# One matrix load per unit, and the next expert's first token blocks transposed one unit earlier

## The chip, the cores and the metric

The kernel runs on one core of a Trainium2 chip. The metric is the device time of one execution in microseconds (us), and the median of several runs is compared.

## The reference

Three stages follow one another on 4608 tokens of 512 numbers. Only the second, the mixture of experts, is touched.

```python
attn_out = _attn_ref(**attn_kwargs)                 # 8 batches, 8 heads, 576 x 64, keys and values pooled by 8
x = attn_out.transpose(0, 2, 1, 3).reshape(B * S, H * D)
...
# second stage: each token goes to its two best experts of eight
for e in range(E):
    for k in range(2):
        mask = top2[:, k] == e
        h = np.maximum(x[mask] @ w1[e], 0.0)        # 512 -> 1024
        out[mask] += top2_w[mask, k, None] * (h @ w2[e])   # 1024 -> 512
...
h = x @ w_in                                        # third stage, 512 -> 2048 -> 512
g = h - np.tanh(h)
return g @ w_out
```

## The kernel before

The second stage walks over 8 experts. An expert has room for 1216 tokens, which are worked on in three groups of 512, 384 and 320 tokens. A group takes 8 units, one for each 128 columns of the expert's hidden layer, so an expert has 24 units, counted here from 0 to 23: units 0 to 7 are the 512 group, 8 to 15 the 384 group, 16 to 23 the 320 group. Numbers are carried as a high and a low half in 16 bits, so a product is three matmuls.

A unit does this, in the order in which the code issues it: `L1(i, f)` multiplies the group's transposed tokens `xTp` with the first matrix (lines 355 to 357, result in `ph`, two buffers), ScalarE (ACT) and VectorE (DVE) turn `ph` into the hidden tile `hT` (lines 359 and 360); then at most one token block of the next group is transposed by `tr`; then `L2` of two units ago multiplies `hT` with the second matrix (lines 377 to 384, result in `py`); at a group's end `Y` scales the `py` tiles into `ys` (three buffers) and stores them to `y_d` (line 409); then the jobs that a table gives to this unit are run (`at` enters them, `run_jobs` issues them).

`tr` works on a block of up to 128 tokens that `gather` has fetched into `xg`. ACT makes the high half in the single buffer `xp` (line 341), DVE the low half (line 342), SyncE's queue (SP) issues a transposing DMA from `xp` into `xTp` (line 343), and GpSimd (POOL) gathers the block after next. `xTp` has two buffers, so a new group's tile takes the place of the tile of two groups before. TensorE (PE) needs all blocks of a group before its first matmul. A group of four blocks had `tr` in units 0, 2, 4 and 6 of the group before it, a group of three in 0, 2 and 5.

Among the jobs of the table: the next expert's first matrix is loaded into `stage` (line 118, four DMAs of 512 KB), its largest entry is found (`amax`, line 127, units 3 to 6, in expert 0 four later), and it is split into halves in `pair` (lines 154 and 159); from unit 13 the same `stage` takes the second matrix (line 120). Meanwhile a piece of the third stage's matrices is loaded (`raw`, lines 225 and 228) and converted. In experts 1 to 4, units 1 and 2, four sums of such pieces are split (lines 290 and 291) into the same three `ys` buffers and stored to `ws_d` (line 293).

All ordinary DMAs here and the transposes go through SP, which issues in program order. A unit's order on each engine is the order of the code; no scheduler moves it.

Of the kernel before, what the change touches and what calls it, by code (L numbers as in the profile page):

```python
# [37 lines left out]
def kernel(ctx, tc, q, k, v, w_gate, w_noise, noise, w1, w2, w_in, w_out, out):  # L38
# [54 lines left out]
    with ExitStack() as st:  # L93
        moe(nc, tc, st, V, z)
# [81 lines left out]
def both(g):  # L176
    for _ in g:
        pass
# [8 lines left out]
def moe(nc, tc, st, V, z):  # L187
# [8 lines left out]
    KD, KF = DM // 128, FF // 128  # L196
# [6 lines left out]
    groups = []  # L203
    for e in range(E):
        c = 0
# [91 lines left out]
    def at(key, f, *a):  # L297
        jobs.setdefault(key, []).append((f, a))

    def run_jobs(key, between):  # L300
        for f, a in jobs.pop(key, []):
            f(*a)
            between()
# [3 lines left out]
    def gather(k):  # L307
        if k < len(blocks):
            e, c, n = blocks[k]
            if k == 6:  # L310
                x = wk.tile([128, 2, DM], F16, name="xp", bufs=1).rearrange("p a n -> p (a n)").bitcast(F32)
            else:
                x = wk.tile([128, DM], F32, name="xg", bufs=2)
            XG[k] = x
            nc.gpsimd.indirect_dma_start(  # L315
                out=x[:n], out_offset=None, in_=x_d[:, :],
                in_offset=bass.IndirectOffsetOnAxis(ap=idx[:n, e, c:c + 1], axis=0))
# [7 lines left out]
    def tr(i, j):  # L325
        if j == 0:
            XTP[i] = wk.tile([128, 2, KD, 512], F16, name="xTp")
        x = XG.pop(first[i] + j)
        n = blocks[first[i] + j][2]
        if i == 1:  # L330
            p = ps.tile([128, KD, 128], F32, name="pt", bufs=2)
            for m in range(KD):
                nc.tensor.transpose(p[:, m, :n], x[:n, 128 * m:128 * m + 128], identf[:n, :n])
            o = XTP[i][:, :, :, 128 * j:128 * j + n]
            nc.scalar.activation(o[:, 0], p[:, :, :n], AF.Copy)
            tt(o[:, 1], p[:, :, :n], o[:, 0], op=OP.subtract)  # L336
            if j < 2:
                gather(7 + j)
            return
        xp = wk.tile([128, 2, DM], F16, name="xp", bufs=1)  # L340
        nc.scalar.activation(xp[:n, 0], x[:n], AF.Copy)
        tt(xp[:n, 1], x[:n], xp[:n, 0], op=OP.subtract)  # L342
        nc.sync.dma_start_transpose(XTP[i].rearrange("p a m n -> p (a m) n")[:, :, 128 * j:128 * j + n],
                                    xp[:n].rearrange("p a n -> p (a n)"))
        gather(first[i] + j + 2)
# [3 lines left out]
    def L1(i, f):  # L349
        e, g, c0, nt = groups[i]  # L350
        w, x = W[e, 1].pair, XTP[i]
        p = ps.tile([128, 512], F32, name="ph", bufs=2)
        for m in range(KD):
            s = slice(128 * f, 128 * f + 128)
            nc.tensor.matmul(p[:, :nt], w[:, 0, m, s], x[:, 0, m, :nt], start=(m == 0), stop=False)  # L355
            nc.tensor.matmul(p[:, :nt], w[:, 0, m, s], x[:, 1, m, :nt], start=False, stop=False)  # L356
            nc.tensor.matmul(p[:, :nt], w[:, 1, m, s], x[:, 0, m, :nt], start=False, stop=(m == KD - 1))  # L357
        h = HC[i, f] = wk.tile([128, 2, 512], F16, name="hT", bufs=5)
        nc.scalar.activation(h[:, 0, :nt], p[:, :nt], AF.Relu)  # L359
        stt(h[:, 1, :nt], p[:, :nt], 0.0, h[:, 0, :nt], op0=OP.max, op1=OP.subtract)  # L360
# [3 lines left out]
    def L2(i, f):  # L364
        e, g, c0, n = groups[i]
        w, h = W[e, 2].pair.rearrange("p a b (c n) -> p a (b c) n", n=DM), HC[i, f]
        nb, half = divmod(n, 128)
        if f == 0:
            if g == 0:
                SC[e] = wk.tile([128, 1], F32, name="ysc")  # L370
                tt(SC[e], W[e, 1].sc[:, 1:2], W[e, 2].sc[:, 0:1], op=OP.mult)
            for j in range(nb + (half > 0)):
                PY[i, j] = ps.tile([128, DM], F32, name="py", bufs=4)
        for j in range(nb):
            s = slice(128 * j, 128 * j + 128)
            p = PY[i, j]
            nc.tensor.matmul(p, h[:, 0, s], w[:, 0, f], start=(f == 0), stop=False)  # L377
            nc.tensor.matmul(p, h[:, 0, s], w[:, 1, f], start=False, stop=False)  # L378
            nc.tensor.matmul(p, h[:, 1, s], w[:, 0, f], start=False, stop=(f == KF - 1))  # L379
        if half and f % 2:  # L380
            terms = [(u, a, b) for u in (f - 1, f) for a, b in ((0, 0), (0, 1), (1, 0))]
            for k, (u, a, b) in enumerate(terms):
                q = 64 * (k % 2)
                nc.tensor.matmul(PY[i, nb][q:q + 64], HC[i, u][:, a, 128 * nb:n], w[:, b, u],
                                 start=(f == 1 and k < 2), stop=(f == KF - 1 and k > 3))
        if not half:
            del HC[i, f]
        elif f % 2:
            del HC[i, f - 1], HC[i, f]
        if f == KF - 1 and i > 0:  # L390
            Y(i)
# [161 lines left out]
    for e in range(E):  # L553
        if e + 1 < E:
            c1, c2 = PR[e + 1, 1], PR[e + 1, 2]
            d = 4 if e == 0 else 0
            at((e, d), c1.load)
            at((e, 7 + d), lambda c=c1: both(c.fin1()))
            at((e, 8 + d), lambda c=c1: both(c.fin2()))
            for c in range(4):  # L560
                at((e, 3 + d + c), c1.amax, c)
                at((e, (12 if d else 10) + c), c1.split, c)
                at((e, 18 + c // 2), c2.amax, c)
                at((e, 22 + c // 2), c2.split, c)
            at((e, 15 if d else 13), c2.load)
            at((e, 20), lambda c=c2: both(c.fin1()))
            at((e, 21), lambda c=c2: both(c.fin2()))
        cv = Conv(e // 4, e % 4)
        for j in range(8):
            u = j + 3 if 0 < e < 5 else (j + 2 if j < 6 else j + 4) if e + 1 < E else (j + 4 if j < 5 else j + 6)  # L570
            if j < 2:
                at((e, j + 2 * (e + 1 == E)), cv.load, j)
            at((e, u), cv.conv, j)
            if j + 2 < 8:
                at((e, u), cv.load, j + 2)
        at((e, 14), cv.stat)
        at((e, 15), cv.fin1)
        at((e, 16), cv.fin2)
        at((e, 16), cv.norm)
        for j in range(4):  # L580
            at((e, 20 + j // 2), cv.split, j)
            if cv.which == 0:
                if j == 0:
                    at((e + 1, 0), cv.combos)
                at((e + 1, 1 + j // 2), cv.split, j, True)
# [11 lines left out]
    for u in range(len(units) + LAG):  # L597
        if u < len(units):
            i, f = units[u]
            L1(i, f)  # L600
            if u < KF:
                gate(4)
            n = -(-groups[i + 1][3] // 128) if i + 1 < len(groups) else 0
            if i > 0:
                for j in range(n):
                    if j * KF // n == f:
                        tr(i + 1, j)
            elif f == KF - 1:
                while not V["idx_loaded"]:
                    gate(10 ** 6, True)  # L610
                for k in range(4, 7):
                    gather(k)
        if u >= LAG and u not in (KF, KF + 1):
            L2(*units[u - LAG])
        if u == KF - 1:
            L2(*units[u - 1])
            L2(*units[u])
            for j in range(n):
                tr(1, j)
        if u in (KF, KF + 1):  # L620
            Y(0, range(2 * (u - KF), 2 * (u - KF) + 2))
        if u > LAG and units[u - LAG - 1][1] == KF - 1 and groups[units[u - LAG - 1][0]][0:2] == (E - 2, len(SIZES) - 1):
            overflow()
        if u in (1, 3):
            V["first"][1].split((u + 3) // 2)
        if u < KF:
            gate(6, u > 1)
        if u == KF + LAG:
            V["early"].close()
            V["pairs"].append(V["ew"].enter_context(tc.tile_pool(name="ew1", bufs=1, side="right")))  # L630
        if u < len(units):
            run_jobs((groups[i][0], KF * groups[i][1] + f), lambda: u < KF and gate(4))
            if u < KF:
                gate(6)
# [1096 lines left out]
```

## Time and profile before

| | |
|---|---|
| median of 3 runs | 1812.55 us (1811.64 to 1812.95) |
| the profiled execution's own time | 1809.6 us |
| its span, first to last instruction | 1807.6 us |
| PE busy | 1754.3 us, 97% |
| DVE, ACT, POOL busy | 1282.7, 940.8, 277.6 us |
| granted TensorE clock, mean | 0.997 |

Busy PE time counts a matmul from its start to its modelled end. Matmuls overlap, so a wait shows as idle time only after the last one's modelled end.

### The profile page before, as it was taken

To read this page: it belongs to the slowest core of one execution; us is meant where nothing else is said; L and a number is where in the kernel's file an instruction comes from. 1 tells how busy PE (TensorE), PEld (TensorE's weight loads), DVE (VectorE), ACT (ScalarE), POOL (GpSimd) and SP (SyncE) were. 2 spreads that over 40 slices of the span, in tenths; PEclk is the share of its full clock that TensorE was granted. 3 is DMA by queue.
4 is the path that set the end of the run, shared out by engine and by line. 5 is a ranking of instruction groups with operands and counts; after the bars stand their busy time and mean duration, and the time that the engine had idled before them with its cause. 6 is when DMAs were issued, how large, how long until landed. Compare 5 with 4: busy or idle time off the path is not lost. (4 is left out here: it accounts for less than half of the span.)

```text
span 1807.6 us, 28937 instructions
## 1 busy us (share of the span) xinstructions
PE 1754.3 (97%) x10791; PEld 1069.2 (59%) x10792; DVE 1282.7 (71%) x2550; ACT 940.8 (52%) x2249; POOL 277.6 (15%) x264
## 2 busy tenths in 40 slices
PE   7999989999999999999999999999999999999998
PEld 5998854445454454545455454566666666666664
DVE  5688786766666766665665457687887879788765
ACT  5887732424434343434334246566665756666554
POOL 2334101302121130100101012010120201010000
PEclk8999999999999999999999999999999999999999
DMA  9867214454655445454634335430322314041100
GB/s 240 220 172 211 79 59 149 120 166 140 198 152 143 131 120 177 140 149 129 149 102 123 100 101 140 103 89 23 94 65 48 95 34 94 18 94 46 37 25 25
DMA packets 264158, 203.45 MB, mean 113 GB/s; under 512 B 188160, under 2 KB 208640, under 8 KB 264000
## 3 DMA queue, kind: packets, MB, share of 16 engines
q1 hardware_dynamic: 251840, 162.16, 33.1%
q0 software_dynamic: 11904, 38.81, 8.2%
q8 instruction: 89, 1.46, 0.3%
q14 instruction: 69, 0.57, 0.1%
q10 hardware_dynamic: 256, 0.46, 0.1%
HBM read 121.82 MB, written 45.74 MB: 93 GB/s over the span
## 5 line engine op out<-in xcount | busy, mean ns | idle before, releaser
L359 ACT ACTIVATE hT<-ph 128x512 f16<-128x512 f32 (+2 forms) x192 | 96.8, 505 | 432.6 <-PE ph L357 432.3
L355 PE MATMUL ph<-xTp,pair 128*128 128x384 f16 (+2 forms) x736 | 245.2, 333 | 15.0 <-DMA xTp<-xp 6.0
L356 PE MATMUL ph<-xTp,pair 128*128 128x384 f16 (+2 forms) x736 | 244.9, 333 | 0.4 <-DVE xTp L336 0.4
L357 PE MATMUL ph<-xTp,pair 128*128 128x384 f16 (+2 forms) x736 | 244.9, 333 | 0.0
L360 DVE SCALAR_TENSOR_TENSOR hT<-ph,hT 128x512 f16<-128x512 f32 (+2 forms) x192 | 110.7, 576 | 166.2 <-ACT hT L359 166.0
L1042 PE MATMUL py<-wo,gT 128*128 128x512 f16 x576 | 218.3, 379 | 1.0 <-DVE gT L989 1.0
L1040 PE MATMUL py<-wo,gT 128*128 128x512 f16 x576 | 218.3, 379 | 0.1
L377 PE MATMUL py<-pair,hT 128*128 128x512 f16 x576 | 218.3, 379 | 0.0
L378 PE MATMUL py<-pair,hT 128*128 128x512 f16 x576 | 218.3, 379 | 0.0
L379 PE MATMUL py<-pair,hT 128*128 128x512 f16 x576 | 218.3, 379 | 0.0
L1041 PE MATMUL py<-wo,gT 128*128 128x512 f16 x576 | 218.3, 379 | 0.0
L315 POOL DMA_INDIRECT xg<-x_d,idx x75 | 85.3, 1137 | 673.5 <-DVE xp L342 462.0
L899 PEld LDWEIGHTS <-wi 128*128 128x128 f16 x1536 | 150.3, 98 | 58.5 <-issue 0.2
L713 POOL DMA_INDIRECT y<-y_d,ridx x64 | 79.3, 1240 | 514.9 <-DVE y L724 240.3
L355 PEld LDWEIGHTS <-pair 128*128 128x128 f16 x768 | 75.0, 98 | 83.0 <-issue 23.2
L356 PEld LDWEIGHTS <-pair 128*128 128x128 f16 x768 | 75.1, 98 | 62.5 <-issue 6.7
L357 PEld LDWEIGHTS <-pair 128*128 128x128 f16 x768 | 75.1, 98 | 57.1 <-issue 0.6
L999 ACT ACTIVATE th<-th,bias 128x512 f32<-128x512 f32 x144 | 102.5, 712 | 3.3 <-DVE th L997 3.3
L1000 DVE SCALAR_TENSOR_TENSOR th<-th,t 128x512 f32<-128x512 f32 x144 | 98.5, 684 | 1.4 <-ACT th L999 1.4
L989 DVE TENSOR_TENSOR gT<-th,gT 128x512 f16<-128x512 f32 x144 | 98.6, 685 | 0.2 <-ACT gT L988 0.2
L996 DVE SCALAR_TENSOR_TENSOR t<-hb,cinf,hs 128x512 f32<-128x512 f32 x64 | 48.0, 749 | 71.0 <-ACT hs L995 71.0
L1042 PEld LDWEIGHTS <-gT 128*128 128x128 f16 x576 | 56.3, 98 | 69.3 <-DVE gT L989 1.5
(306 smaller groups left out, 3499.1 us busy)
## 6 DMA issues: line engine op xcount, KB each, us to landing
stage<-in_moe_w SPq DMA_DIRECT2D x64, 512.0 KB, 6.4
y_d<-ys SPq DMA_DIRECT2D x82, 256.0 KB, 2.1
x_d<-xr SPq DMA_DIRECT2D x36, 256.0 KB, 2.3
out<-o SPq DMA_DIRECT2D x36, 256.0 KB, 2.6
qt<-in_q SPq DMA_DIRECT2D x32, 256.0 KB, 6.2
raw<-in_moe_w_in SPq DMA_DIRECT2D x32, 256.0 KB, 3.3
raw<-in_moe_w_out SPq DMA_DIRECT2D x32, 256.0 KB, 3.3
kt<-in_k SPq DMA_DIRECT2D x7, 768.0 KB, 5.4
```

Of the source, the lines that this page charges most:

```text
L355: nc.tensor.matmul(p[:, :nt], w[:, 0, m, s], x[:, 0, m, :nt], start=(m == 0), stop=False)
L356: nc.tensor.matmul(p[:, :nt], w[:, 0, m, s], x[:, 1, m, :nt], start=False, stop=False)
L357: nc.tensor.matmul(p[:, :nt], w[:, 1, m, s], x[:, 0, m, :nt], start=False, stop=(m == KD - 1))
L360: stt(h[:, 1, :nt], p[:, :nt], 0.0, h[:, 0, :nt], op0=OP.max, op1=OP.subtract)
L377: nc.tensor.matmul(p, h[:, 0, s], w[:, 0, f], start=(f == 0), stop=False)
L378: nc.tensor.matmul(p, h[:, 0, s], w[:, 1, f], start=False, stop=False)
L379: nc.tensor.matmul(p, h[:, 1, s], w[:, 0, f], start=False, stop=(f == KF - 1))
L899: nc.tensor.matmul(p, w[:, a, m], y[:, c, b, m], start=(start and m + x == 0), stop=(m == 1 and x == 2), skip_group_check=True)
L999: nc.scalar.activation(q, q, AF.Square, bias=bias[:, 2:3], scale=SP5)
L1040: nc.tensor.matmul(p, g[:, 0, s], wo[:, 0, f], start=(f == 0), stop=False)
L1041: nc.tensor.matmul(p, g[:, 0, s], wo[:, 1, f], start=False, stop=False)
L1042: nc.tensor.matmul(p, g[:, 1, s], wo[:, 0, f], start=False, stop=(f == KF - 1))
```

## The change

The first matrix's four loads are issued one in each of four units (0 to 3, in expert 0 units 4 to 7) where all four stood in the first of these. And where the next group is a new expert's 512 group, its four blocks are transposed in unit 7 of the 384 group and in units 1, 3 and 5 of the 320 group, so in units 15, 17, 19 and 21 of the expert where it was 16, 18, 20 and 22.

```diff
@@ -554,7 +554,8 @@
         if e + 1 < E:
             c1, c2 = PR[e + 1, 1], PR[e + 1, 2]
             d = 4 if e == 0 else 0
-            at((e, d), c1.load)
+            for c in range(4):
+                at((e, d + c), c1.load, [c])
             at((e, 7 + d), lambda c=c1: both(c.fin1()))
             at((e, 8 + d), lambda c=c1: both(c.fin2()))
             for c in range(4):
@@ -603,8 +604,10 @@
             n = -(-groups[i + 1][3] // 128) if i + 1 < len(groups) else 0
             if i > 0:
                 for j in range(n):
-                    if j * KF // n == f:
+                    if (2 * j - 1 if n == 4 else j * KF // n) == f:
                         tr(i + 1, j)
+                if f == KF - 1 and i + 2 < len(groups) and groups[i + 2][1] == 0:
+                    tr(i + 2, 0)
             elif f == KF - 1:
                 while not V["idx_loaded"]:
                     gate(10 ** 6, True)
```

PE's rows are the same in both programs. On SP, from the second matrix's loads in expert 0 (line 120) to unit 2 of expert 1, the rows before are:

```order
L120 DMA stage<-in_moe_w 128x2x512 x4
L343 DMA_TRANSPOSE xTp<-xp 128x8x128
L409 DMA y_d<-ys 128x512 x3
L343 DMA_TRANSPOSE xTp<-xp 128x8x128 x4
L118 DMA stage<-in_moe_w 128x1024 x4
L225 DMA raw<-in_moe_w_in 128x512
L409 DMA y_d<-ys 128x512 x2
L409 DMA y_d<-ys 64x512
L293 DMA ws_d<-ys 256x1x512 x2
L225 DMA raw<-in_moe_w_in 128x512
L343 DMA_TRANSPOSE xTp<-xp 128x8x128
```

and now:

```order
L343 DMA_TRANSPOSE xTp<-xp 128x8x128
L120 DMA stage<-in_moe_w 128x2x512 x4
L343 DMA_TRANSPOSE xTp<-xp 128x8x128
L409 DMA y_d<-ys 128x512 x3
L343 DMA_TRANSPOSE xTp<-xp 128x8x128 x3
L118 DMA stage<-in_moe_w 128x1024
L225 DMA raw<-in_moe_w_in 128x512
L409 DMA y_d<-ys 128x512 x2
L409 DMA y_d<-ys 64x512
L293 DMA ws_d<-ys 256x1x512 x2
L118 DMA stage<-in_moe_w 128x1024
L225 DMA raw<-in_moe_w_in 128x512
```

One load instead of four stands ahead of the last group's three stores to `y_d`, the next load behind the first two stores to `ws_d`; and in expert 0 the first of the four transposes has moved ahead of the second matrix's loads (in later experts those are issued in unit 13, ahead of it in both programs).

On ACT, units 15 to 17 of expert 1 (line 359 with 128x384 is unit 14 or 15, with 128x320 a unit of the 320 group), before:

```order
L359 ACTIVATE hT<-ph 128x384 x2
L359 ACTIVATE hT<-ph 128x320
L341 ACTIVATE xp<-xg 128x512
L359 ACTIVATE hT<-ph 128x320
L405 ACTIVATE ys<-py,ysc 128x512
```

and now:

```order
L359 ACTIVATE hT<-ph 128x384 x2
L341 ACTIVATE xp<-xg 128x512
L359 ACTIVATE hT<-ph 128x320 x2
L341 ACTIVATE xp<-xg 128x512
L405 ACTIVATE ys<-py,ysc 128x512
```

The first block's high half moved from unit 16 to 15, the second's from unit 18 to 17, where it stands ahead of the 384 group's evictions.

On ACT, units 20 to 22 of expert 1, where the last two blocks are made, before:

```order
L341 ACTIVATE xp<-xg 128x512
L290 ACTIVATE wi<-qf,wsc 128x512 x2
L359 ACTIVATE hT<-ph 128x320
L290 ACTIVATE wi<-qf,wsc 128x512 x2
L359 ACTIVATE hT<-ph 128x320
L341 ACTIVATE xp<-xg 128x512
L154 ACTIVATE pair_5146<-stage,wsc 128x1024 x2
```

and now:

```order
L359 ACTIVATE hT<-ph 128x320
L290 ACTIVATE wi<-qf,wsc 128x512 x2
L359 ACTIVATE hT<-ph 128x320
L341 ACTIVATE xp<-xg 128x512
L290 ACTIVATE wi<-qf,wsc 128x512 x2
L359 ACTIVATE hT<-ph 128x320
L154 ACTIVATE pair_5146<-stage,wsc 128x1024 x2
```

The last block's high half stands one `hT` eviction earlier, ahead of the second pair of `wi` splits.

## Rows read from the trace of the kernel before

**Rows 1.** The page's first part: busy us (share of span), PE's entry in its line.

```profile
PE 1754.3 (97%) x10791; PEld 1069.2 (59%) x10792; DVE 1282.7 (71%) x2550; ACT 940.8 (52%) x2249; POOL 277.6 (15%) x264
```

**Rows 2.** Waits of PE: who waited for whom: us in total, times, longest us.

```profile
PE ph L355 <- DMA xTp<-xp: 6.0, 5, 1.5
...
PE ph L355 <- DVE hT L360: 4.7, 3, 1.8
...
PE ph L355 <- DVE pair L159: 2.3, 2, 1.2
PE pt L170 <- DVE cm L130: 1.7, 2, 1.4
```

**Rows 3.** PE's timeline at unit 0 of expert 2, then at its unit 2.

```profile
461.58 0.84 PE L384 MATMUL py<-pair,hT 128*64 128x512 f16 x6
463.88 0.38 PE L355 MATMUL ph<-xTp,pair 128*128 128x512 f16 x1 [1.47 <-DMA xTp<-xp]
...
471.74 0.84 PE L384 MATMUL py<-pair,hT 128*64 128x512 f16 x6
472.51 0.39 PE L355 MATMUL ph<-xTp,pair 128*128 128x512 f16 x1
```

**Rows 4.** Line 343 from 459.0 to 459.3 us: issue, and its time to landing.

```profile
L343 SPq DMA_TRANSPOSE xTp<-xp x1: 1232/1232/1232, 459.2 to 459.2; - x1
...
DMA to landing us min/median/max: 4.5/4.5/4.5
```

**Rows 5.** ACT's timeline in units 21 and 22 of expert 1.

```profile
453.36 0.44 ACT L359 ACTIVATE hT<-ph 128x320 f16<-128x320 f32 x1 [0.86 <-PE ph L357]
...
457.46 0.44 ACT L359 ACTIVATE hT<-ph 128x320 f16<-128x320 f32 x1 [2.45 <-PE ph L357]
457.80 0.62 ACT L341 ACTIVATE xp<-xg 128x512 f16<-128x512 f32 x1
```

**Rows 6.** DVE's timeline in unit 21 of expert 1.

```profile
453.83 0.49 DVE L360 SCALAR_TENSOR_TENSOR hT<-ph,hT 128x320 f16<-128x320 f32 x1 [0.31 <-ACT hT L359]
455.73 0.16 DVE L101 TENSOR_SCALAR wsc<-pt 128x1 f32<-128x1 f32 x1 [1.41 <-PE pt L183]
```

**Rows 7.** Lines 118 and 409 at the start of expert 1: issues, time to landing.

```profile
L118 SPq DMA_DIRECT2D stage<-in_moe_w x4: 430/502/583, 364.9 to 366.5; - x4
...
DMA to landing us min/median/max: 6.1/7.1/8.6
...
L409 SPq DMA_DIRECT2D y_d<-ys x3: 517/654/664, 367.9 to 369.9; - x3
...
DMA to landing us min/median/max: 7.4/8.3/8.4
```

**Rows 8.** ACT's timeline in units 1 and 2 of expert 1.

```profile
376.33 0.72 ACT L290 ACTIVATE ys<-qf,wsc 128x512 f16<-128x512 f32 x1 [5.74 <-DMA y_d<-ys]
...
377.94 0.58 ACT L359 ACTIVATE hT<-ph 128x512 f16<-128x512 f32 x1
```

**Rows 9.** PE's timeline at unit 4 of expert 1.

```profile
377.65 0.38 PE L379 MATMUL py<-pair,hT 128*128 128x512 f16 x1
379.48 0.38 PE L355 MATMUL ph<-xTp,pair 128*128 128x512 f16 x1 [1.45 <-DVE hT L360]
379.69 0.38 PE L356 MATMUL ph<-xTp,pair 128*128 128x512 f16 x1
```

**Rows 10.** Waits of ACT, whole span.

```profile
ACT ys L290 <- DMA y_d<-ys: 22.2, 4, 6.0
```

**Rows 11.** Line 120 in unit 13 of expert 1: issues, time to landing.

```profile
L120 SPq DMA_DIRECT2D stage<-in_moe_w x4: 388/460/722, 427.0 to 428.5; - x4
...
DMA to landing us min/median/max: 4.3/6.7/7.8
```

**Rows 12.** ACT's timeline in units 15 and 17 of expert 1.

```profile
431.41 0.49 ACT L359 ACTIVATE hT<-ph 128x384 f16<-128x384 f32 x1 [3.40 <-PE ph L357]
...
440.02 0.44 ACT L359 ACTIVATE hT<-ph 128x320 f16<-128x320 f32 x1 [3.98 <-PE ph L357]
```

**Rows 13.** Tile xTp, whole span: time from issue to landing of its 73 transposes.

```profile
DMA to landing us min/median/max: 2.6/4.3/10.2
```

## The prediction

> **What bounds the kernel now.** I read the page's busy line first: PE is busy 97% of the span [rows 1], and its rows are the same in both programs, so the change can only give back PE's idle time or add to it. Then PE's waits, for the second stage. Four rows matter [rows 2]: the first matmul of a unit (line 355) waits 6.0 us in 5 places for a transpose, 2.3 us in 2 for a split of DVE, 4.7 us in 3 for `hT`, and line 170 1.7 us in 2 for the largest entry of a matrix.
>
> Five and two make seven, and there are seven expert starts (1 to 7). The timeline of one shows the pattern [rows 3]: the last group's matmuls are issued, then PE stands 1.47 us until the fourth block has landed. That block's transpose is issued at 459.2 and takes 4.5 us [rows 4], so it lands at 463.7; PE starts at 463.88. In the two starts put down to line 159 that split only happens to end there: it writes the second matrix's halves, which no matmul of unit 0 reads. I count them with the others: 6.0 + 2.3 = 8.3 us idle.
>
> The waits for `hT` lie in unit 4 of experts 1, 2 and 4. Followed back in expert 1: unit 4's `L1` needs the `ph` buffer of unit 2, whose eviction on ACT starts only at 377.94, because ACT stood 5.74 us before line 290, until a store to `y_d` had landed [rows 8]; PE pays 1.45 us [rows 9]. Line 290 needs a `ys` buffer, and the three of them still hold the last group's output. Experts 1 to 4 all have this ACT wait (22.2 us in 4) [rows 10]; in one of them it is short enough to cost PE almost nothing. The stores are late because four loads of 512 KB stand ahead of them: the loads land 6.1 us after the first issue and 8.6 after the last, so at 371.0 and 375.1, and the first store, issued at 367.9, at 376.3 [rows 7].
>
> **The change part by part.**
>
> *Nothing is added or dropped.* The same loads, gathers, conversions and transposes are issued; only their places on SP, ACT, DVE and POOL change. So there is no new work to price, only waits.
>
> *Blocks one unit earlier.* The fourth block moves from unit 22 to 21. Before, the transpose is issued 459.2 - 457.46 = 1.74 us after the unit's eviction starts on ACT [rows 4, 5]. In unit 21 that eviction starts at 453.36 [rows 5], and DVE has a hole of 1.41 us before 455.73 [rows 6], into which its half of the block, after the eviction at 453.83, fits. So the transpose is issued at about 455.1 and, with the same 4.5 us, lands at 459.6. PE would come to its first matmul, without the wait, at 463.88 - 1.5 = 462.4: a margin of 2.8 us. The wait goes away as a whole. What it is worth is a little more than its idle time, because idle counts only from the modelled end of the last matmul: with the wait the two rows start 463.88 - 461.58 = 2.30 us apart, without it 472.51 - 471.74 = 0.77 [rows 3], a difference of 1.53 for 1.47 idle. Seven starts: 8.3 + 7 x 0.06 = 8.7 us.
>
> *What the earlier blocks push.* Each engine's order is fixed, so I looked at who stands behind the moved work. Unit 15's transpose writes the `xTp` buffer that unit 15's own `L1` has just read; SP must wait for those matmuls, but ACT makes `xp` only after that unit's eviction, which itself waits for them: no new wait. `xp` is one buffer; successive blocks stay two units apart, some 8 us at 4.1 a unit [rows 5], against a median landing of 4.3 us [rows 13]. The tight place is unit 17: the first block's transpose now stands behind the second matrix's loads, which land by 428.5 + 7.8 = 436.3 [rows 11]. It is issued at 431.41 + 1.74 = 433.2 [rows 12], so lands between 433.2 + 4.3 = 437.5 and, if it takes its 4.5 us only after the loads, 440.8; ACT wants `xp` again at 440.02 + 0.34 = 440.4 [rows 5, 12]. ACT waits 0 to 0.4 us there, which its idle 3.98 us before unit 17's eviction and the two `ph` buffers absorb. I take 0. The gathers keep their distance of two blocks.
>
> *One load per unit.* Ahead of the `y_d` stores now stands one load instead of four. Spaced (375.1 - 371.0) / 3 = 1.37 us apart [rows 7], three loads are 4.1 us: the first store lands at about 372.2, ACT's line 290 starts there and not at 376.33, the eviction of unit 2 at about 373.8 and not at 377.94 [rows 8]. PE waited only 1.45 us idle, so 2.6 us remain as margin, and the wait goes. Start to start it is worth 379.48 - 377.65 = 1.83 us against 379.69 - 379.48 = 0.21 for neighbours without a wait, so 1.62 for 1.45 idle [rows 9]; three of them: 4.7 + 3 x 0.17 = 5.2 us. The other side: loads two to four come one to three units later, but `amax` reads each three units after its own issue, as the first one before; a unit of the 512 group is 24 matmuls at 0.21, so 5 us [rows 9], and a load takes 8.6 at the longest [rows 7]. What hides them is thus some 15 us; if a load came after that, DVE would stand before `amax`, and `hT` behind it. Expert 0's loads, later by up to three units, have the same three units. I take 0 for these.
>
> A rule of the Trainium skill speaks against this part. In DMA: Bandwidth & Descriptors, section Queues, rings and completion order, it says that descriptors are taken in ring order but that completion is not FIFO per issuing engine, so a later DMA may be done before an earlier one. By that a store need not wait for the loads ahead of it, the lateness would have another cause, and the sum would be 8.9 instead of 14.1 us. Here the stores land after the last load (376.3 after 375.1 us), which agrees with ring order.
>
> *The small one.* The two waits of line 170 for `cm` (1.7 us, the longer 1.4) [rows 2] lie in expert 0. The longer is before the moved work. For the other, 0.3 us, DVE's half of a block moves from unit 18 to 19 but stays ahead of the last `amax`; between 0 and 0.3, I take 0.2.
>
> **Sum.** 8.7 + 5.2 + 0.2 = 14.1 us off the profiled execution's own 1809.6, so 1795.5. The median of the runs is 1812.55, 2.95 above that execution, so 1798.4.
>
> **The rivals.**
>
> 1. *The stores stay late.* If it is the stores themselves, or ACT's line 290 then waits as long for another `ys` buffer (the next one holds a store to `ws_d`, and the second load now stands behind that), only the starts are won: 8.7 + 0.2, so 1803.7. For it: ACT has one more such buffer to wait for. Against: the loads' and the stores' landings follow each other at once, and the margin is 2.6 us.
> 2. *The starts are half won.* The block in unit 21 comes behind DVE's `wsc` work, if ACT's half is late and misses the 1.41 us hole: then it is issued after 456.4, lands after 460.9, still ahead of 462.4. It needs another 1.5 us to cost anything. With half of the starts' wait left: 14.1 - 4.4 = 9.7, so 1802.9.
> 3. *No change.* Something ready just behind the transposes holds PE at the same moment. The order shows nothing of that kind: what the second matrix's splits write is first read by the `L2` of unit 2, two units on. 1812.5.
> 4. *Slower.* ACT stands before `xp` in unit 17, since the first block's transpose now follows the second matrix's loads, and holds the 384 group's evictions behind it, until PE lacks a `py` or `ph` buffer. PE is covered by about a unit, 457.46 - 453.36 = 4.1 us [rows 5]. To lose 14.1 + 3.6 us over the six experts that load in unit 13 (1 to 6), each must lose 3.0, so the transpose would have to land at 440.4 + 4.1 + 3.0 = 447.5, 14.3 us after issue; the longest of 73 took 10.2 [rows 13]. Then 1816 or more. From 444.5 on it would begin to cost.
>
> **How the numbers follow.** Both waits gone, 1796.5 to 1800: 72%. Rival 1, 11%; rival 2, 8%; rival 3, 6%; rival 4, 3%. The range that leaves out rivals 3 and 4 and keeps rivals 1 and 2 is 1796.0 to 1804.5; its low end also has the chance that waits I priced at nothing, such as the short one in expert 3, go too. A measurement of this kernel can tell about 0.2%, 3.6 us, from no change; the first three cases lie beyond it: faster 91%, same 6%, slower 3%.
>
> **What would show each step.** In the changed kernel's PE waits, line 355 should no longer wait for a transpose or for line 159 at seven starts (a few tenths in all), nor for line 360 in units 4. The fourth block's transpose should be issued some 7 us ahead of the new expert's first matmul, and the first store to `y_d` of experts 1 to 4 should land about 4 us sooner after its issue than 8.4 us. ACT's wait of line 290 for `y_d`, 22.2 us, should fall to below 6. I am wrong if ACT's line 341 gains waits of several us in unit 17, if line 290 waits as long for `ws_d`, or if DVE stands before `amax` for `stage`.

## The result, and the profile after

The changed kernel took 1797.22 us (median of 6 runs, 1794.80 to 1798.16) against 1811.53 us before (6 runs): a ratio of 0.9919, 95% interval 0.9907 to 0.9931. It is 14.3 us faster; 14.1 us were forecast, to 1798.4 us. By the interval the gain lies between 12.5 and 16.8 us, so that the two agree to 0.2 us is in part luck.

Waits of PE in the changed kernel, the longest sums first (engine, line waited for: us in total, times, longest us):

```profile
PE px L1370 <- DVE lg L1387: 5.7, 4, 2.5
PE pt L1252 <- DVE vm L1248: 4.1, 1, 4.1
PE pt L1281 <- DVE ke L1238: 2.7, 1, 2.7
PE pt L170 <- DVE cm L130: 1.6, 2, 1.4
```

Three rows of [rows 2] are missing, the ones of line 355 for the transposes, for line 159 and for `hT`. What heads the list now lies in the first stage. The start of expert 2, PE's timeline, beside [rows 3]:

```profile
461.25 0.84 PE L384 MATMUL py<-pair,hT 128*64 128x512 f16 x6
462.02 0.39 PE L355 MATMUL ph<-xTp,pair 128*128 128x512 f16 x1
```

The two rows stand 0.77 us apart, as at a place without a wait, where they stood 2.30 apart before. The fourth block's transpose in the same expert, line 343, issue and landing, beside [rows 4]:

```profile
L343 SPq DMA_TRANSPOSE xTp<-xp x1: 1232/1232/1232, 454.7 to 454.7; - x1
...
DMA to landing us min/median/max: 4.4/4.4/4.4
```

It landed at 459.1, 2.9 us ahead of PE. The first store to `y_d` of expert 1, line 409, beside [rows 7]:

```profile
L409 SPq DMA_DIRECT2D y_d<-ys x1: 326/326/326, 368.2 to 368.2; - x1
...
DMA to landing us min/median/max: 4.9/4.9/4.9
```

4.9 us from issue to landing, where it was 8.4. It was also issued 1.0 us sooner after the expert's first matmul, because three of the loads no longer occupy SP ahead of it. ACT's waits for a `ys` buffer and for `xp`, whole span, beside [rows 10]:

```profile
ACT ys L290 <- DMA y_d<-ys: 4.6, 4, 1.5
...
ACT ys L290 <- DMA ws_d<-ys: 4.2, 4, 1.7
ACT xp L341 <- DMA xTp<-xp: 4.1, 2, 3.1
```

The wait for `y_d` fell from 22.2 to 4.6 us. Of the kernel before, the other two were:

```profile
ACT xp L341 <- DMA xTp<-xp: 5.1, 3, 3.8
...
ACT ys L290 <- DMA ws_d<-ys: 4.8, 5, 1.7
```

Neither grew, and the two waits for `xp` now lie in unit 5 of experts 1 and 2, none in unit 17: two of the three signs of being wrong that the prediction names did not come. The third did, DVE's wait for `stage`; it is taken up below.

The two profiled executions differ by less, 1809.6 against 1798.16, because the first stage took longer in the second one. First matmuls of the second stage (`x0T`) and of the third, before and then after (the number before "to" is the first start):

```profile
L355 PE MATMUL ph<-x0T,pair x32: 376/379/389, 249.1 to 285.2; 128*128 128x512 f16 x32
...
L771 PE MATMUL ph<-stage,wi x60: 376/379/389, 1087.0 to 1153.8; 128*128 128x512 f16 x60
```

```profile
L355 PE MATMUL ph<-x0T,pair x32: 376/379/389, 252.0 to 288.2; 128*128 128x512 f16 x32
...
L774 PE MATMUL ph<-stage,wi x60: 376/379/389, 1075.4 to 1142.8; 128*128 128x512 f16 x60
```

The second stage went from 1087.0 - 249.1 = 837.9 us to 1075.4 - 252.0 = 823.4, so 14.5 us. The first stage, whose code is the same, took 2.9 us more in the second execution: its 1812 matmuls kept PE busy 227.7 us and not 225.0, at a granted clock of 0.97 and not 0.98. So medians of several runs are compared below, and single waits.

### The profile page after: what moved, and what is told of

It reads as the page before. It is cut to its first block, busy times and chain, and to the rows that moved or that the text cites. A ratio compares the mean times of both kernels' runs of the same rounds, so it can differ in the third digit from the quotient of the medians.

```text
span 1795.9 us, 28933 instructions
## 1 busy us (share of the span) xinstructions
PE 1756.3 (98%) x10792; PEld 1071.3 (60%) x10792; DVE 1284.9 (72%) x2550; ACT 939.9 (52%) x2249; POOL 269.8 (15%) x264
## 5 line engine op out<-in xcount | busy, mean ns | idle before, releaser
L315 POOL DMA_INDIRECT xg<-x_d,idx x75 | 77.6, 1035 | 666.9 <-DVE xp L342 508.8
```

## The experiments

The theory: two separate waits were removed. At seven expert starts PE waited for the landing of the fourth block; in unit 4 of experts 1, 2 and 4 it waited, over ACT, for stores that stood behind three loads too many. The rivals: one part did all of it, or the parts work only together, or all the blocks matter and not only the fourth, or the stores were late for another reason than their place in the ring.

### Only the loads

```diff
-            at((e, d), c1.load)
+            for c in range(4):
+                at((e, d + c), c1.load, [c])
```

> Only the loads are spread; the blocks are transposed where they were. If the two waits are separate, PE's waits in unit 4 go and the seven at the expert starts stay at about 8.3 us idle: 5.2 to 5.5 us off, so 1806.1 against 1811.5 before. If the burst of loads is also what makes the fourth block late, the starts go too and the time is near 1797.

Measured: 1806.18 us, ratio 0.9974 (0.9965 to 0.9983). PE's waits of line 355 in it:

```profile
PE ph L355 <- DMA xTp<-xp: 4.7, 4, 1.4
...
PE ph L355 <- DVE pair L159: 3.9, 3, 1.4
```

4.7 + 3.9 = 8.6 us in 4 + 3 = 7 places: all the starts are back. The row for `hT` is gone. That the releaser of three of the seven is now line 159, where it was two, with nothing changed there, fits the reading that this name is a coincidence of times.

### Only the transposes

```diff
+                    if (2 * j - 1 if n == 4 else j * KF // n) == f:
+                        tr(i + 1, j)
+                if f == KF - 1 and i + 2 < len(groups) and groups[i + 2][1] == 0:
+                    tr(i + 2, 0)
```

> Only the blocks are moved; the four loads stand together in unit 0. If the two waits are separate, the seven starts go and three waits in unit 4 stay at about 4.7 us idle: 8.8 to 9.1 us off, so 1802.6. If the parts only work together, less than 6 us is won.

Measured: 1802.32 us, ratio 0.9959 (0.9945 to 0.9972). No start waits, and

```profile
PE ph L355 <- DVE hT L360: 3.9, 4, 1.7
```

The waits in unit 4 stay. The two parts alone are worth 1811.14 - 1806.18 = 5.0 and 1811.14 - 1802.32 = 8.8 us, together 13.8, beside 14.3 for the whole: they add up, within what the intervals allow.

### Only the fourth block earlier

```diff
-                    if (2 * j - 1 if n == 4 else j * KF // n) == f:
+                    if (5 if n == 4 and j == 3 else j * KF // n) == f:
                         tr(i + 1, j)
-                if f == KF - 1 and i + 2 < len(groups) and groups[i + 2][1] == 0:
-                    tr(i + 2, 0)
```

> Loads spread as in the changed kernel; of the four blocks only the fourth is moved, from unit 22 to 21, the others stay in 16, 18 and 20. If only the landing of the fourth block counts: ACT waits some 1.5 us for the single xp in unit 21, the transpose is issued near 456.7 on the clock of the kernel before and lands near 461.2, still ahead of the 462.4 at which PE arrives, so the starts stay free of waits and the time is that of the changed kernel, 1797 to 1799. If the blocks must move together because xp is single, more than half of the start waits comes back: 1802 or more.

Measured: 1797.35 us, ratio 0.9922 (0.9908 to 0.9936), the same as the changed kernel. ACT's timeline in unit 21 of expert 1:

```profile
451.71 0.44 ACT L359 ACTIVATE hT<-ph 128x320 f16<-128x320 f32 x1 [0.86 <-PE ph L357]
453.59 0.63 ACT L341 ACTIVATE xp<-xg 128x512 f16<-128x512 f32 x1 [1.45 <-DMA xTp<-xp]
```

ACT waits 1.45 us for the single `xp`, as worked out, and PE doesn't notice, except once. ACT's and PE's rows ahead of expert 6 and at its start:

```profile
860.96 0.63 ACT L341 ACTIVATE xp<-xg 128x512 f16<-128x512 f32 x1 [3.17 <-DMA xTp<-xp]
```

```profile
867.10 0.38 PE L355 MATMUL ph<-xTp,pair 128*128 128x512 f16 x1 [0.68 <-DVE pair L159]
```

There the third block's transpose took 4.8 us to land, where it took 3.0 to 3.1 at the six other starts. ACT stood 3.17 us for `xp`, the fourth block's transpose was issued 1.4 to 1.8 us later than elsewhere, and PE waited 0.68 us for it. So the moves of the first three blocks bring no time that can be measured; they spare ACT the wait for the single `xp` and keep the margin, which without them was used up at one start of seven.

### The fourth block back in its place

```diff
-                    if (2 * j - 1 if n == 4 else j * KF // n) == f:
+                    if ((-1, 1, 3, 6)[j] if n == 4 else j * KF // n) == f:
```

> The changed kernel with the fourth block back in unit 22, the first three in 15, 17 and 19. If only the fourth block's landing counts, all seven start waits are back at about 8.3 us idle, near 1806.5. If the earlier blocks themselves bring something, under 6 us idle.

Measured: 1805.62 us in one run, and

```profile
PE ph L355 <- DMA xTp<-xp: 4.7, 4, 1.5
...
PE ph L355 <- DVE pair L159: 3.5, 3, 1.2
```

8.2 us in seven places. With the run before this settles it: the start wait is the fourth block's landing. The others matter only in so far as the fourth must wait for `xp` behind them.

This run also shows the mechanism of the slower rival, in expert 0 (ACT's row in unit 19, then PE's):

```profile
344.50 0.63 ACT L341 ACTIVATE xp<-xg 128x512 f16<-128x512 f32 x1 [2.01 <-DMA xTp<-xp]
```

```profile
348.36 0.27 PE L170 MATMUL pt<-identf,cm 128*1 128x128 f32 x1 [1.25 <-DVE cm L130]
```

The second block's transpose, issued behind the second matrix's loads, took 7.2 us to land; ACT stood 2.0 us for `xp`, DVE's half and the searches behind it came later, and line 170 waited 1.25 us, where it had waited 0.3.

### The fourth block another unit later

```diff
-                    if (2 * j - 1 if n == 4 else j * KF // n) == f:
+                    if ((-1, 1, 3, 7)[j] if n == 4 else j * KF // n) == f:
```

> The same with the fourth block in unit 23. If the start wait is the fourth block's landing and nothing else, each of the seven waits grows by one unit of the 320 group, about 3 us: 8.3 to 29 us idle, near 1827. If another wait stands close behind, or the landing time shrinks with a free queue, clearly less than 20 us is added.

Measured: 1831.45 us in one run, 25.8 more than with the block in unit 22. The idle time before line 355 grew less than forecast:

```profile
PE ph L355 <- DMA xTp<-xp: 16.3, 5, 3.4
...
PE ph L355 <- DVE pair L159: 6.4, 2, 3.2
```

22.7 us in seven places, 14.5 more, so 2.1 a start and not 3. The transpose was issued 3.3 us later, but it landed after 3.0 us, where with the block in unit 22 it took 4.1 to 4.6. In expert 2 SP's queue held nothing else beside it in either run. What differs is the gather that GpSimd issues beside it: its issue took 1.86 us in unit 23 and 0.94 in unit 22, and the two transfers landed together in unit 22 (expert 2: 463.6 and 463.8 us) but 1.4 us apart in unit 23; that this is the cause is not shown. The other 11 us are not idle time. PE's timeline at the start of expert 1 in this kernel:

```profile
362.00 0.38 PE L355 MATMUL ph<-xTp,pair 128*128 128x512 f16 x1 [3.35 <-DMA xTp<-xp]
362.22 0.38 PE L356 MATMUL ph<-xTp,pair 128*128 128x512 f16 x1
...
364.26 0.63 PE L357 MATMUL ph<-xTp,pair 128*128 128x512 f16 x1
364.69 0.64 PE L355 MATMUL ph<-xTp,pair 128*128 128x512 f16 x1
...
372.32 0.39 PE L355 MATMUL ph<-xTp,pair 128*128 128x512 f16 x1
```

The matmuls begin 0.22 us apart and go on 0.43 apart. The first 4 us of experts 1, 3 and 4 (PE's busy time, and behind the bracket the granted clock):

```profile
362.00:366.00 4.00, 4.00 (x13) 0.65 0.12 45
576.65:580.65 4.00, 4.00 (x19) 1.00 0.13 49
681.83:685.83 4.00, 4.00 (x10) 0.50 0.14 54
```

In expert 1 the clock was granted at half, 1.2 GHz, for part of it. From unit 0 to unit 2 it took 372.32 - 362.00 = 10.32 us; before it took 472.51 - 463.88 = 8.63 [rows 3]. That is 1.69 us more. Five of the seven starts lost as much; expert 3 lost nothing, and expert 4, where the clock stood at half already when PE resumed, 2.75. That makes 11.2 us, and with the 14.5 us idle 25.7, beside 25.8 measured, closer than two single runs need agree. So the theory of the wait stands, and my price for a longer one was wrong in both its parts.

### Three loads, then one

```diff
-            for c in range(4):
-                at((e, d + c), c1.load, [c])
+            at((e, d), c1.load, [0, 1, 2])
+            at((e, d + 1), c1.load, [3])
```

> The changed kernel, but three loads in the first unit and the fourth in the next. If the stores to y_d wait in ring order behind the loads, one load less takes some 1.4 us from each of ACT's four waits for y_d (22.2 us before, so about 16.5), and PE keeps what was above that: 0.2, 0.6 and 0.2 us in three units 4. If any break of the burst is enough, ACT's wait falls to about 5 and PE has none; if the loads don't matter, both stay as before (22.2 and 4.7).

Measured: 1797.98 us in one run. Of PE's and ACT's waits:

```profile
PE ph L355 <- DVE hT L360: 2.6, 3, 1.2
```

```profile
ACT ys L290 <- DMA y_d<-ys: 19.3, 5, 5.7
```

The waits lie between the two rivals' forecasts. The run with only the transposes is the nearer comparison, since it has the same blocks and four loads together:

```profile
ACT ys L290 <- DMA y_d<-ys: 21.7, 4, 5.8
```

PE's waits fell from its 3.9 us to 2.6 (1.0 was forecast), and ACT's from 21.7 to 19.3, 0.6 us for each of the four experts where 1.4 was forecast. But that is a mean of very unequal differences: ACT's wait grew by 0.5 us in expert 1 and fell by 2.2 in expert 3. Two executions with the same loads, the kernel before and the run with only the transposes, already differ by up to 1.3 us in one expert. So fewer loads ahead mean an earlier store, but what one load costs is not settled by this one execution.

Nor are the loads' landings evenly spaced. In expert 1 the second load was issued at 364.3 and landed after 7.0 us, the third at 364.8 and landed after 8.9: 2.4 us apart, although 1.37 us was the mean over a burst of four [rows 7]. In that burst the landings are 1.27, 1.26 and 1.55 us apart. In most bursts, of four and of three, the last load is the slow one. I don't know why.

### The loads together, on ACT's queue

```diff
-                self.nc.sync.dma_start(self.stage[:, c], src[128 * c:128 * c + 128, :])
+                (self.nc.scalar if self.e > 1 else self.nc.sync).dma_start(self.stage[:, c], src[128 * c:128 * c + 128, :])
```

> The kernel before, with the four loads still together in unit 0, but in experts 1 to 6 issued by ACT and not by SP. If the stores are late because they stand behind the loads in one ring, ACT's wait for y_d falls from 22.2 us to under 8, PE's waits in unit 4 go, the starts stay: about 5 us off. If they are late because all transfers share the same DMA engines, the stores still end with the loads: ACT's wait stays near 20 us and PE's near 4.7.

Measured: 1806.51 us in one run. ACT's wait for the stores, and PE's behind it:

```profile
ACT ys L290 <- DMA y_d<-ys: 17.0, 5, 4.3
```

```profile
PE ph L355 <- DVE hT L360: 1.3, 1, 1.3
```

PE's loss fell from 4.7 to 1.3 us, but ACT still waited 17.0 us, and the transpose just ahead of the stores in SP's ring, in expert 1, took 8.5 us to land. So a burst on another ring still slows what is in flight, and part of the stores' lateness was shared DMA engines, not only the order of the ring. The Trainium skill says in DMA: Bandwidth & Descriptors, section Issuing engines are not separate DMA queues, that DMAs of all issuing engines run on the same engines and interleave; the 8.5 us agree.

What the fall from 4.7 to 1.3 us is due to, this run doesn't show, because it changed the time of the loads as well as their ring. The first matmul of expert 1 in it, and the loads:

```profile
359.62 0.38 PE L355 MATMUL ph<-xTp,pair 128*128 128x512 f16 x1 [1.32 <-DVE pair L159]
```

```profile
L118 ACTq DMA_DIRECT2D stage<-in_moe_w x4: 352/444/453, 362.5 to 363.9; - x4
...
DMA to landing us min/median/max: 3.7/5.3/8.3
```

On ACT the first load is issued 2.9 us after the first matmul; on SP, in the kernel before, it stands behind a transpose and is issued 6.1 us after it (358.86, and 364.9 by [rows 7]). So the burst starts 3.2 us sooner, its last load lands 3.7 us sooner after the first matmul, and the first store 2.3 us sooner, still behind the last load. The earlier burst alone could have given that. Loads on ACT's ring that are issued no sooner were not tried.

### Two small waits more

```diff
-                at((e, 3 + d + c), c1.amax, c)
+                at((e, (6 if d else 3) + c), c1.amax, c)
...
-    at((2, 1), clear)
+    at((5, 4), clear)
```

> The changed kernel, with the eleven zero stores to y_d moved from expert 2's unit 1 to expert 5's unit 4, and expert 0's four searches of the first matrix's largest entry one unit earlier. If the new wait in expert 2 comes from the third and fourth load standing behind those stores, DVE's 3.3 us before amax go and PE's line 170 there waits no more (0.2 us idle, 0.4 start to start). If the 1.4 us of line 170 in expert 0 come from the search being held behind an eviction that waits for y_d, they go as well. Together about 2 us less than the changed kernel, 1795.2; if neither, 1797.2. So small a step is to be seen in the waits rather than in the time.

Measured: 1795.47 us, ratio 0.9905 (0.9890 to 0.9921), against 0.9919 for the changed kernel: the intervals overlap, and by time alone the two can't be told apart. The waits can. The changed kernel has two waits that the kernel before had not, DVE for a load of `stage`, 0.89 us in expert 1 and 2.42 in expert 2, together 3.3. That of expert 2 (DVE's timeline, then SP's ahead of it):

```profile
496.51 1.22 DVE L127 TENSOR_REDUCE am<-stage 128x1 f32<-128x1024 f32 x1 [2.42 <-DMA stage<-in_moe_w]
```

```profile
479.26 8.38 SPq L593 DMA_DIRECT2D y_d<-ys  x11
487.74 1.34 SPq L343 DMA_TRANSPOSE xTp<-xp  x1
...
490.64 1.23 SPq L118 DMA_DIRECT2D stage<-in_moe_w  x2
```

Eleven zero stores, issued in expert 2's unit 1, hold SP for 8.4 us, and the third and fourth load come only behind them; PE pays 0.24 us at line 170. With the stores moved, that wait is gone, and with the search one unit earlier so is the 1.4 us wait of line 170 in expert 0. The wait in expert 1 stays, for no zero stores stand there. It is 0.90 us in this run, and in the changed kernel:

```profile
390.94 1.22 DVE L127 TENSOR_REDUCE am<-stage 128x1 f32<-128x1024 f32 x1 [0.89 <-DMA stage<-in_moe_w]
```

There the third load was issued at 379.9, behind the second pair of stores to `ws_d`, and took 11.0 us to land. So the forecast that all of the 3.3 us would go was wrong by the part of expert 1.

One wait of line 170 is left in this execution, in expert 6:

```profile
PE pt L170 <- DVE cm L130: 0.5, 1, 0.5
```

There the first block's transpose, issued at 938.4 behind the second matrix's loads, took 7.1 us to land and ACT stood 0.9 us for `xp`, which fits the mechanism of my slower rival, at a small price.

## Why the prediction was right, and where it was off

- **The starts, 8.7 us.** Right in mechanism and size: alone 8.8 us. The transpose was forecast to land 2.8 us ahead of PE and landed 2.9 ahead. Whether PE waits is decided by the fourth block's landing. The price of a unit of the 320 group, 4.1 us, came from one pair of rows and is too high: in expert 6 of the changed kernel the four transposes are issued 7.6, 6.9 and 6.4 us apart, not 8. Against a landing of 4.4 us that was still enough.
- **The stores, 5.2 us.** Right in size: alone 5.0 us. The store was forecast to land 4.1 us sooner; in expert 1 it landed 3.5 us sooner after its issue and was issued 1.0 us sooner, which the prediction did not count. The step behind it, that each load ahead costs the same 1.37 us, is not borne out: with one load less ACT's waits fell by 0.6 us on average, unevenly, and the last load of a burst mostly lands late. Nor is the order of the ring all of it: with the loads on another ring ACT's wait was still 17.0 us, between 22.2 before [rows 10] and 4.6 with the loads spread. The gain came out all the same, because it takes less than the three loads gave: PE needed 1.45 us of them in expert 1.
- **What I priced at nothing.** "Loads two to four come one to three units later" was taken as covered by 15 us. It is not: DVE before `amax`, a sign of being wrong by the prediction's own words, waited 3.3 us in two places, and PE 0.24. In expert 2 I didn't count the eleven zero stores that stand ahead of the third and fourth load on SP. In expert 1 the third load stands behind stores to `ws_d`: DVE came for it 10.2 us after its issue, not 15, and it took 11.0 us to land, not 8.6 at the longest. The transpose ahead of it in that expert, issued 1.2 us after the second load, took 11.5 us, where it had taken 4.9; that cost ACT 1.0 us and PE nothing.
- **Line 170, 0.2 us.** The short wait in expert 0 went; the one in expert 2 came. Nothing is left of the term.
- **The slower rival.** ACT's waits for `xp` after the second matrix's loads are not there in the profiled execution of the changed kernel. In other runs with the blocks moved they are; the longest are 2.0 us in expert 0 with the fourth block back in unit 22 and 0.9 in expert 6 with the two small waits removed, and PE's line 170 waited 1.25 and 0.5 us behind them. The evictions were covered, as forecast; the search for the largest entry was not, and the prediction did not look at it.
- **Completion not in order.** This rule of the Trainium skill (DMA: Bandwidth & Descriptors, section Queues, rings and completion order) stood beside rival 1. The landings on SP's ring come in the order of issue: in the trace of the kernel before, none of SP's 553 DMAs landed ahead of one issued before it. So the rival had no ground in this kernel.

What is open: why the last load of a burst mostly lands later than its place says, what one load ahead costs a store, how much of the stores' lateness is the ring's order and how much the shared DMA engines, and why the third block's transpose took 4.8 us ahead of expert 6.

## What to carry to other kernels

When PE is busy 97% of the time, look for waits that repeat once per outer step, find the one item that lands last in each, and ask by how much; here moving that one item by one slot was enough, and the rest of the batch hardly mattered. A large load doesn't cost only its own consumers: it costs whatever small store or transpose is issued behind it, so spread loads over the time that they have, and then check the places where something else already fills the queue. And when an experiment moves work to another queue, check whether the work also starts at another time; if it does, the run can't tell the two apart.

## What the hardware showed beside that

A wait of PE can cost more than its length. Waits of 1.0 to 1.5 us at the seven starts of the kernel before left the granted clock at full speed; of the 4.2 us after the longest one, in expert 2:

```profile
463.80:468.00 4.20, 4.12 (x20) 1.00 0.00 0
```

With the fourth block in unit 23 PE stood 3.20 to 3.35 us, and the clock was granted at half at six of the seven starts. In expert 1 that came after the work had resumed: the matmuls were 0.22 us apart at first, and from about 1.1 us on 0.43, so that two units lost 1.69 us more. In expert 4 it came before PE resumed and cost 2.75 us. In expert 3, with 3.24 us idle, it did not come at all. So the same wait cost between nothing and 2.75 us on top of itself. The Trainium skill describes this in TensorE: Matmul & The Clock Gate, Part 1, as a clock gate that lowers the clock after idling; six of the seven starts agree.
